# Rows of G for the first four chunks by three transfers, one gate range for them, and a new order of the first 830 steps

## The chip, the core and the metric

The kernel runs on one core of a Trainium2 chip. Its engines work side by side, each through its own queue in order: PE (TensorE) multiplies matrices, DVE (VectorE), ACT (ScalarE) and POOL (GpSimd) do element-wise work, SP issues most DMAs; ACT issues some. The metric is the device time of one execution in microseconds; less is better.

## The reference

Three stages follow each other. For 4 batches, 8 heads, 768 steps and head size 40, a recurrence with exponential gates:

```
m_new = max(f[t] + m, i[t]);  fs = exp(f[t] + m - m_new);  is = exp(i[t] - m_new)
C = fs*C + is * v[t] k[t]^T;  n = fs*n + is*k[t]
y[t] = sigmoid(o[t]) * (C q[t]) / max(|n . q[t]|, 1)
```

The outputs, 3072 tokens of 320 numbers, go through two feed-forward stages with 2048 hidden units: `h = x @ w_in; g = h*clip(h+3, 0, 6)/6; x = g @ w_out`, and the same with `g = max(h, 0)**2`. The result has 3072 x 320 numbers.

## The kernel before, in words

The recurrence is done in 12 chunks of 64 steps. A unit is one batch and one chunk; there are 48, and the first eight are chunks 0 and 1 of batches 0 and 1 and then of batches 2 and 3. For a unit, `at_load` fetches q and k transposed (`qkt`), k (`kI`) and v (`Z`); `at_S` (L431, L433) multiplies q with k into PSUM; `at_P` (L455) multiplies that by the gate weights W; `x_k` (L403, L406) scales k; `at_Y` (L473) multiplies with v and the carried state; `at_C` (L481) carries the state on; `at_n1`, `at_n2`, `at_n3` normalise and multiply by the sigmoid of the o gate (`o_load`, `o_sig`) into X.

W is exp(G[t] - G[s] + ...), with G the running sum of gate logs. A range of chunks goes through `gate_m` (a max-scan), `gate_g`, `gate_G` (a sum-scan), `gate_b` and `gate_bT` on 32 partitions, one for each batch and head. Before, the ranges are chunks 0-1, 2-3 and 4-11. For the first four chunks (units 0 to 15) G is split into two parts of 32-bit "r" format, high and low, in the tile Gp, and `w_pe` forms the exponent on PE: the first matmul (L353) writes the causal mask, the second (L355) adds, with `gb[:, c]` as stationary and R[b] as moving operand, the b terms through 64 rows that select the head (`head_rows`) and G through two rows of ones. R and gb lie in the tile `pre`. Each unit's two rows of R[b] are loaded by `at_gload`: two DMAs on ACT's queue, 32 in all for 16 units. `w_e` (L375) takes the exponential on ACT. Later units get W by a broadcast DMA from DRAM.

The feed-forward stages work in slots: `mm_A` (L619, eight matmuls of w_in into PSUM), `act1`, `act1b`, `act2`, `act2b` (L628 to L650: the activation and its split into a high part `gh` and a low part `gl`), then `mm_B` (L660). The first 16 slots take half the tokens each. X is transposed by `t_pe` (L595) and split by `t_hi`, `t_lo` into `xs`, and mm_A:0 needs the transposes of batches 0 and 1, that is units 0 to 3. The weights come as 64-bit floats: `w_load` (768 or 640 KB), `w_exp` (ACT), `w_b1`, `w_b2` (DVE), `w_hi` (ACT or DVE), `w_lo` (POOL or DVE).

The order of all of it is written out by hand in the text FIRST, step by step (`name:arguments`, and `@v`, `@g`, `@a` for DVE, POOL or ACT where a step may run on several); behind its last step a rule continues. Each engine runs its instructions in that order. Each DMA takes the next of eight completion lanes (DMAHW0 to 7) in turn and waits, on the queue of the engine that issues it, until the lane's last DMA has landed.

Of the kernel before, what the change touches and what calls it, by code (L numbers as in the profile page):

```python
# [38 lines left out]
w_e:2 w_b2:0,0 w_load:0,4 w_e:3 w_pe:4 x_k:2@v w_hi:0,0 w_pe:5 at_P:2,0 w_exp:0,2 w_lo:0,0 at_n1:1
at_Y:2 at_n2:1 at_load:5 w_e:5 at_n1:2 w_e:4 w_b1:0,2 w_exp:0,1 w_load:0,3 at_S:3 at_n2:2 x_k:3  # L40
at_gload:7 at_gload:6 at_gload:8 at_P:3,0 at_gload:9 at_C:2 at_n3:2 at_Y:3 at_load:6 at_n3:1
t_pe:0,0,0 at_n1:3 at_C:3 t_hi:0,0,0 at_n2:3 w_pe:6 w_load:0,6 at_n3:3 w_pe:7 w_exp:0,4 w_b2:0,2
w_e:6 t_lo:0,0,0 w_e:7 w_hi:0,2@v t_pe:0,0,1 at_gload:11 w_load:0,5 at_gload:10 w_b1:0,1 t_hi:0,0,1
t_lo:0,0,1 w_exp:0,3 w_lo:0,2@v mm_A:0 w_load:0,7 w_b2:0,1 mm_A:1 act1:0 w_b1:0,4 w_hi:0,1 at_S:4
act1b:0 x_k:4 act1:1 act2:0 act1b:1 w_lo:0,1 at_load:7 act2b:0 act2:1 act2b:1 w_exp:0,6 mm_A:2
at_P:4,0 w_load:0,8 mm_A:3 w_b2:0,4 act1:2 at_S:5 w_b1:0,3 w_hi:0,4 act1b:2 x_k:5 mm_B:0,1 act1:3
at_P:5,0 at_Y:4 w_exp:0,5 at_load:8 w_lo:0,4 act1b:3 mm_B:0,0 act2:2 at_n1:4 at_S:6 at_C:4 act2b:2
load_gates:1 act2:3 at_n2:4 x_k:6 w_exp:0,7 mm_A:4 at_P:6,0 at_load:9 w_b1:0,6 mm_B:1,0 act1:4
at_Y:5 w_b2:0,6 mm_B:1,1 w_load:0,10 at_n1:5 at_C:5 at_S:7 w_hi:0,6 x_k:7@v act2b:3 w_exp:0,8
w_lo:0,6 at_load:10 at_P:7,0 mm_A:5 act1b:4 w_pe:8 at_n2:5 act2:4 w_load:0,9 act1:5 act2b:4 at_Y:6  # L50
w_e:8 act1b:5 mm_A:6 w_b2:0,3 at_gload:12 at_C:6 at_n1:6 w_hi:0,3 at_S:8 w_load:0,12 at_n3:4 act1:6
at_n2:6 w_lo:0,3 x_k:8@a act1b:6 at_Y:7 at_P:8,0 at_n3:6@g at_n1:7 mm_B:2,0 mm_B:2,1 at_C:7@v
at_load:11 mm_B:3,1 w_exp:0,10 w_b1:0,5 t_pe:0,0,2 w_b2:0,5 mm_B:3,0 t_hi:0,0,2 at_n3:5 act2:5
w_load:0,11 w_hi:0,5 at_n2:7 at_n3:7 at_Y:8 act2:6 act2b:5 w_lo:0,5 w_exp:0,9 o_load:1 act2b:6
mm_A:7 at_C:8 t_lo:0,0,2 w_b1:0,7 t_pe:0,0,3 act1:7 mm_B:4,1 w_b2:0,7 w_exp:0,12 mm_B:4,0
w_load:0,13 mm_B:5,0 act1b:7 t_hi:0,0,3 mm_B:5,1 w_b1:0,8 w_hi:0,7 t_lo:0,0,3 act2:7 w_lo:0,7
act2b:7 mm_A:8 w_load:0,14 at_n1:8 at_n2:8 mm_A:9 w_exp:0,11 w_b2:0,8 act1:8 mm_B:6,1 act1:9
mm_B:6,0 act1b:8 w_hi:0,8 act1b:9 mm_B:7,0 gate_m:2 mm_B:7,1 o_load:2 act2:8 w_pe:9 act2:9 o_sig:1
act2b:8 w_lo:0,8 act2b:9 mm_B:8,3 mm_A:10 w_e:9 o_load:3 at_gload:13 gate_g:2 mm_A:11 w_exp:0,13
act1:10 mm_B:8,2 act1:11 act1b:10 at_n3:8@g mm_B:9,2 act1b:11 act2:10 mm_B:9,3 act2b:10 w_pe:10  # L60
w_exp:0,14 gate_G:2 mm_A:12 w_e:10 mm_B:10,3 act1:12 mm_B:10,2 at_gload:14 act2:11@v at_S:9 x_k:9
o_sig:2 act2b:11 act1b:12 mm_A:13 at_P:9,0 at_load:12 act2:12 act2b:12 mm_B:11,2 act1:13 w_b1:0,10
at_S:10 o_sig:3 act1b:13 x_k:10 mm_A:14 at_P:10,0 act2:13 at_load:13 act2b:13 mm_B:12,2 act1:14
mm_B:11,3 w_b2:0,10 mm_A:15 act1b:14 w_hi:0,10 gate_b:2 w_pe:11 act2:14 mm_B:12,3 w_e:11 at_Y:9
act2b:14 w_lo:0,10 o_load:5 act1:15 w_pe:12 at_gload:15 act1b:15 at_C:9 mm_A:16 at_n1:9 act2:15
act2b:15 w_e:12 w_b1:0,9 w_b2:0,9 mm_A:17 act1:16 w_load:0,15 gate_bT:2 w_hi:0,9 act1b:16 o_load:4
w_lo:0,9 at_S:11 act1:17 at_n2:9 mm_B:13,2 act1b:17 at_Y:10 x_k:11 at_P:11,0 mm_B:13,3 w_b1:0,12
at_C:10 at_load:14 at_S:12 act2:16 w_b1:0,11 act2b:16 x_k:12 mm_B:14,3 w_exp:0,15 mm_B:14,2
at_P:12,0 at_load:15 mm_A:18 act2:17 w_b2:0,12 act2b:17 w_hi:0,12 w_pe:13 at_n3:9 act1:18 mm_A:19
w_b2:0,11 w_e:13 act1b:18 w_lo:0,12 w_hi:0,11 at_n1:10 w_pe:14 act1:19 at_n2:10 mm_B:15,2 mm_B:16,2  # L70
w_e:14 act1b:19 w_lo:0,11 at_Y:11 w_pe:15 at_gload:16 at_n1:11 at_C:11 mm_B:15,3 w_add:16 w_e:15
mm_B:16,0 act2:18 mm_B:16,3 mm_B:16,1 at_n3:10 at_n2:11@a at_S:13 act2b:18 w_mask:16 w_b1:0,14
mm_A:20 at_P:13,0 x_k:13 w_e:16 w_b2:0,14 at_load:16 act2:19 at_Y:12 act1:20 act2b:19 mm_B:17,1
at_gload:17 at_C:12 at_S:14 x_k:14 at_n1:12 w_hi:0,14 at_n2:12 mm_B:18,1 at_n3:12 at_load:17
at_Y:13 at_P:14,0 w_lo:0,14 mm_B:17,0 act1b:20 at_C:13 at_gload:18 t_pe:0,1,0 at_n1:13 mm_B:17,2
t_hi:0,1,0@v mm_B:17,3 x_q:16 mm_B:18,2 t_lo:0,1,0 act2:20 mm_B:18,3 mm_B:19,3 act2b:20 w_add:17
mm_A:21 at_n3:11 at_n2:13 w_mask:17 mm_B:19,2 act1:21 at_n3:13 at_Y:14 act1b:21 w_add:18 w_e:17
t_pe:0,1,1 at_C:14 mm_A:22 at_n1:14 w_mask:18 t_hi:0,1,1@v at_n2:14@a t_lo:0,1,1 mm_B:18,0
w_b1:0,13 at_S:15 w_b2:0,13 act2:21 w_b1:0,15 mm_B:19,0 w_e:18 at_P:15,0 x_k:15 mm_B:19,1 act1:22
act2b:21 at_S:16 x_k:16 at_load:18 w_hi:0,13 at_Y:15 act1b:22 at_n3:14@g mm_A:23 at_P:16,0 act2:22  # L80
at_gload:19 at_P:16,1 at_C:15 at_load:19 at_n1:15 w_lo:0,13 at_n2:15 act2b:22 at_S:17 act1:23
at_gload:20 at_Y:16 w_b2:0,15 mm_B:20,2 at_C:16 x_q:17@v mm_B:20,0 w_hi:0,15 mm_B:21,0 at_n1:16
at_n3:15@g mm_B:20,3 at_n2:16 mm_B:21,2 at_P:17,0 w_lo:0,15 mm_B:20,1 at_P:17,1 mm_B:21,1 act1b:23
t_pe:0,1,2 mm_B:21,3 act2:23 x_k:17@v mm_B:22,1 t_hi:0,1,2 act2b:23 w_add:19 mm_B:22,2 at_load:20
at_Y:17 t_lo:0,1,2 w_mask:19 mm_B:22,3 at_gload:21 at_n1:17 at_C:17 t_pe:0,1,3 at_n2:17 mm_B:22,0
x_q:18 w_e:19 mm_B:23,0 t_hi:0,1,3 mm_B:23,1 evac:23,0 t_lo:0,1,3 mm_B:23,2 at_n3:17@g evac:23,1
mm_B:23,3 evac:23,2 mm_A:24 evac:23,3 x_k:18@v at_n3:16 x_q:19 mm_A:25 act1:24 act1b:24 x_k:19
act2:24 at_S:18 w_add:20 mm_A:26 act1:25 at_P:18,1 at_load:21 act1b:25 w_add:21 act2:25@v mm_A:27
act2b:24 act2b:25 act1:26 at_P:18,0 w_mask:20 mm_B:24,2 act1b:26 act1:27 at_gload:22 at_Y:18
w_mask:21 act2:26@v w_e:20 mm_B:25,2 at_C:18 act2b:26 at_S:19 w_e:21 mm_B:24,0 at_n1:18 x_q:20  # L90
at_load:22 mm_B:24,3 at_n2:18 mm_A:28 at_P:19,0 at_P:19,1 w_add:22 act1b:27 mm_B:24,1 x_k:20@v
at_gload:23 act1:28 mm_B:25,0 at_n3:18@g mm_B:25,3 act2:27 act1b:28 at_Y:19 act2b:27 at_S:20
at_C:19 at_n1:19 x_q:21 mm_B:26,0 qk_split:22 at_load:23 mm_A:29 mm_B:26,2 act1:29 at_P:20,1
w_mask:22 mm_B:26,3 at_n2:19 mm_B:27,3 w_add:23 w_e:22 act1b:29 mm_B:27,2 mm_A:30 at_P:20,0
at_gload:24 x_k:21@v qk_split:23 at_Y:20 at_S:21 at_C:20 mm_B:25,1 at_load:24 at_n1:20 at_n3:19@g
mm_B:26,1 act2:28 mm_B:27,1 at_P:21,1 mm_B:27,0 act2:29@v x_q:22 mm_A:31 at_n2:20 at_P:21,0
at_gload:25 act2b:28 at_S:22 act2b:29 act1:30 mm_B:28,3 act1b:30 w_mask:23 act1:31 mm_B:28,2
mm_B:28,0 qk_split:24 mm_A:32 w_e:23 mm_B:28,1 at_P:22,0 x_k:22 mm_B:29,1 mm_B:29,0 act2:30@v
w_add:24 mm_B:29,3 at_load:25 act1b:31 at_Y:21 act2:31 at_n3:20 mm_A:33 act2b:31 act2b:30
at_gload:26 t_pe:0,2,0 at_n1:21 w_mask:24 act1:32 mm_B:30,0 at_n2:21 mm_B:30,1 act1:33 x_q:23  # L100
act1b:32 mm_B:30,3 w_e:24 mm_B:31,0 at_C:21@v mm_A:34 at_n3:21 t_hi:0,2,0@v x_k:23 act1b:33
w_add:25 at_load:26 mm_B:31,1 t_lo:0,2,0 mm_B:31,3 at_Y:22 w_mask:25 at_S:23 at_n1:22 at_C:22
w_add:26 mm_A:35 w_e:25 at_n2:22 at_P:23,0 qk_split:25 at_gload:27 t_pe:0,2,1 mm_B:29,2 t_hi:0,2,1
mm_B:30,2 act2:32 mm_B:31,2 x_q:24@v at_Y:23 act2b:32 at_C:23 act2:33@v x_q:25 mm_B:32,2 act1:34
# [745 lines left out]
```

## Time and profile before

| what | value |
|---|---|
| runs, median (lowest to highest) | 859.5 us (857.76 to 860.44) |
| profiled execution, its span | 858.58 us, 856.8 us |
| PE busy | 820.4 us, 96% of the span |
| DVE, ACT, POOL busy | 534.0, 415.5, 205.8 us |
| HBM read and written | 58.36 and 4.00 MB |

The busy time of PE is near the span, so that the time of the kernel is PE's work plus what PE waits, and the places to look at are those where PE is idle or its clock is lowered. A wait that the profile shows on another engine counts only if PE's next instruction stands behind it.

### The profile page before, as it was taken

The page shows a single profiled execution, that of the slowest core. Times are in us where ns is not written, and L with a number is a line of the kernel's source. Part 1 is how long each engine was busy: PE and PEld are TensorE (multiplying, and loading weights), DVE is VectorE, ACT ScalarE, POOL GpSimd, SP SyncE. Part 2 cuts the span into 40 slices and gives each one's busy share as a digit, 9 for nine tenths or more (in the row PEclk, how much of TensorE's full clock was granted, in tenths as well). Part 3 has the DMA queues.
Part 4 walks back from the last instruction along what each step waited for, and adds up shares of the span by engine and source line. Part 5 has one row for each costly group of instructions (what it writes and reads, how often), then busy time and mean ns, then how long its engine had stood idle before and what let it go on. Part 6 is the DMA issues. An engine that isn't in the chain of part 4 may idle for free.

```text
span 856.8 us, 19209 instructions
## 1 busy us (share of the span) xinstructions
PE 820.4 (96%) x7968; PEld 724.2 (85%) x7968; DVE 534.0 (62%) x963; ACT 415.5 (48%) x727; POOL 205.8 (24%) x188
## 2 busy tenths in 40 slices
...
GB/s 193 185 139 314 41 148 90 66 138 79 91 83 107 99 92 116 83 105 62 2 37 157 188 160 1 1 31 1 1 32 1 31 1 1 31 1 1 31 1 31
DMA packets 29188, 63.66 MB, mean 74 GB/s; under 512 B 5261, under 2 KB 17613, under 8 KB 29101
## 3 DMA queue, kind: packets, MB, share of 16 engines
...
q8 instruction: 62, 1.02, 0.5%
...
q10 hardware_dynamic: 512, 0.07, 0.1%
HBM read 58.36 MB, written 4.00 MB: 73 GB/s over the span
## 4 chain that ended last, share of the span: by engine, by line
PE 83%; DVE 5%; DMA 4%; ACT 4%; issue 2%; SPq 2%; ACTq 0%; POOL 0%; POOLq 0%; DVEq 0%
PE hps L619 38%; PE acc L660 36%; PE Yp L473 3%; PE tp L595 2%; PE Sp L439 2%; DMA qkt<-in_qk 1%; DVE qs L417 1%; DMA rwi<-in_w1i 1%; ACT qs L415 1%; PE Sp L431 1%; PE Sp L433 1%; DMA rwo<-in_w1o 1%; DVE X L512 1%; DMA pre<-Gp 0%; DVE Xm L455 0%
## 5 line engine op out<-in xcount | busy, mean ns | idle before, releaser
L619 PE MATMUL hps<-xs,wi 128*128 128x512 f32 (+1 forms) x1600 | 392.1, 389 | 4.0 <-DVE gl L650 3.1
L660 PE MATMUL acc<-wo,gh 128*128 128x320 f32 x1536 | 349.1, 314 | 0.0
L619 PEld LDWEIGHTS hps<-xs,wi 128*128 128x128 f32 x1600 | 289.3, 192 | 54.4 <-DVE gl L650 3.5
L660 PEld LDWEIGHTS acc<-wo,gh 128*128 128x128 f32 x1536 | 259.3, 189 | 10.1
L660 PE MATMUL acc<-wo,gl 128*128 128x320 f32 x768 | 237.9, 310 | 0.0
L650 DVE TENSOR_TENSOR gl<-g,gh 128x512 fp32r<-128x512 f32 x176 | 128.2, 730 | 65.9 <-ACT gh L645 64.9
L640 DVE TENSOR_TENSOR g<-g 128x512 f32<-128x512 f32 x96 | 66.4, 692 | 127.6 <-ACT g L630 127.1
L660 PEld LDWEIGHTS acc<-wo,gl 128*128 128x128 f32 x768 | 144.6, 188 | 0.2
L628 ACT ACTIVATE g<-hps,three 128x512 f32<-128x512 f32 (+1 forms) x104 | 67.8, 654 | 152.5 <-PE hps L619 140.6
L645 ACT CAST gh<-g 128x512 fp32r<-128x512 f32 x168 | 104.1, 619 | 67.5 <-DVE g L640 53.3
L630 ACT ACTIVATE g<-hps 128x512 f32<-128x512 f32 x96 | 57.4, 598 | 151.5 <-PE hps L619 151.5
L637 DVE SCALAR_TENSOR_TENSOR g<-g,hps 128x512 f32<-128x512 f32 x80 | 54.8, 686 | 53.3 <-ACT g L628 53.0
L395 POOL TENSOR_TENSOR Xm<-qkt,W 40x512 f32<-40x512 f32 x29 | 38.3, 1321 | 111.8 <-ACT W L385 77.4
L580 POOL TENSOR_TENSOR wi<-wt,wi 128x768 fp32r<-128x768 f32 x15 | 29.7, 1979 | 128.5 <-ACT wi L575 125.5
L473 PEld LDWEIGHTS Yp<-Z,Xm 104*32 104x32 f32 (+1 forms) x3072 | 35.0, 109 | 20.4 <-issue 12.4
L473 PE MATMUL Yp<-Z,Xm 104*32 104x41 f32 (+1 forms) x3072 | 41.1, 208 | 6.9 <-DVE Xm L455 4.6
L417 DVE SCALAR_TENSOR_TENSOR qs<-qs,less,qkt 120x512 fp32r<-120x512 f32 x52 | 39.4, 799 | 11.1 <-ACT qs L415 11.0
L362 POOL TENSOR_TENSOR W<-W,bT 104x512 f32<-104x512 f32 x32 | 44.3, 1386 | 1.5 <-DMA W<-Gd 1.4
L406 POOL TENSOR_TENSOR Xm<-kI,W 104x320 f32<-104x320 f32 x37 | 33.6, 909 | 31.0 <-ACT W L375 21.0
L580 POOL TENSOR_TENSOR wo<-wt,wo 128x640 fp32r<-128x640 f32 x16 | 26.0, 1626 | 49.0 <-ACT wo L575 46.4
L512 DVE TENSOR_TENSOR X<-X,yt 64x320 f32<-64x320 f32 x39 | 32.6, 836 | 1.1
L481 ACT COPY Z<-Yp 40x328 f32<-40x328 f32 x41 | 17.4, 427 | 30.5 <-PE Yp L473 11.1
(102 smaller groups left out, 652.1 us busy)
## 6 DMA issues: line engine op xcount, KB each, us to landing
...
```

What stands on the lines that cost most here:

```text
L362: on("w_add", "g", u).tensor_tensor(out=W, in0=W, in1=bT[:, c - NC1, b * H:(b + 1) * H].unsqueeze(2).to_broadcast([KX, H, L]), op=ALU.add)
L417: nc.vector.scalar_tensor_tensor(out=y[0:KS, i], in0=y[0:KS, i].bitcast(F32), scalar=less[0:KS, i:i + 1], in1=x[0:KS, i], op0=ALU.mult, op ...
L473: nc.tensor.matmul(out=Yp[o:e, h, :], lhsT=Xm[:, h, o:e], rhs=Z[b][c % 2][:, h, :], start=True, stop=True)
L580: on("w_lo", "g", ph, i).tensor_tensor(out=w[:, 1], in0=f, in1=w[:, 0].bitcast(F32), op=ALU.subtract)
L619: nc.tensor.matmul(out=h, lhsT=w[:, hl, kk, o:o + P], rhs=t[:, xk, i0 * P:i1 * P], start=(i == 0), stop=(i == len(TERMS) - 1))
L628: nc.scalar.activation(out=g, in_=T["h", s], func=ACTF.Relu, bias=three)
L630: nc.scalar.activation(out=g, in_=T["h", s], func=ACTF.Relu)
L637: nc.vector.scalar_tensor_tensor(out=g, in0=r, scalar=6.0, in1=T["h", s], op0=ALU.min, op1=ALU.mult)
L640: nc.vector.tensor_tensor(out=g, in0=r, in1=r, op=ALU.mult)
L645: copy("act2", s)(out=gh, in_=g)
L650: nc.vector.tensor_tensor(out=gl, in0=g, in1=gh.bitcast(F32), op=ALU.subtract)
L660: nc.tensor.matmul(out=acc[i], lhsT=g[:, n], rhs=w[:, hl, m % MG, :], start=(m == 0 and q == 0), stop=(m == NM - 1 and q == 2))
```

## The change

Chunks 0 to 3 become one gate range (`cuts = [0, NC1, NC]` with NC1 = 4), so that the scans run once over 256 columns. Gp's two halves are stored to a DRAM tile Gd1 by two DMAs (`at_G:0,0` and `at_G:0,1`), and one DMA (`at_R:0`) loads all rows for all batches: R[b] has eight rows of G, high and low of four chunks, instead of two. The stationary operand selects the chunk: `gb` has a block with ones only in the two rows of its chunk, made by `const_o` from the identity. The 32 loads of `at_gload` for units 0 to 15 are gone. FIRST has 829 steps instead of 845, in a new order; it holds the same steps but for those of the gates.

```diff
-const_g load_gates:0 const_z:0 const_i at_load:0 head_rows:1 at_load:1 const_z:1 head_rows:0
+const_z:3 const_i load_gates:0 const_g const_k:0 const_m head_rows:2 const_z:1 w_load:0,4 const_z:0
...
+    Gd1 = dram.tile([NC1, 2, BH * L], F32, name="Gd1")
...
-    cuts = [0, 2, 4, NC]
+    cuts = [0, NC1, NC]
...
-    KW = 2 * BH + 2
+    KW = 2 * BH + 2 * NC1
...
-        nc.vector.memset(gb[2 * BH:KW].bitcast(F32), 1.0)
...
+        k = slice(2 * BH, KW)
+        nc.vector.tensor_tensor(
+            out=gb[k],
+            in0=ident[k, 2 * BH:KW:2].unsqueeze(2).to_broadcast([2 * NC1, NC1, KX]),
+            in1=ident[k, 2 * BH + 1:KW:2].unsqueeze(2).to_broadcast([2 * NC1, NC1, KX]),
+            op=ALU.add)
...
+    def at_G(r, i):
+        c0, c1 = cuts[r], cuts[r + 1]
+        nc.scalar.dma_start(
+            out=Gd1[c0:c1, i].rearrange("c (h l) -> c h l", l=L),
+            in_=Gp[:, i, c0 * L:c1 * L].bitcast(F32).rearrange("h (c l) -> h c l", l=L))
+
+    def at_R(r):
+        c0, c1 = cuts[r], cuts[r + 1]
+        k = 2 * BH + 2 * c0
+        nc.scalar.dma_start(
+            out=pre[k:k + 2 * (c1 - c0), 0:B].bitcast(F32),
+            in_=Gd1[c0:c1].rearrange("c i (b k) -> (c i) b k", b=B))
+
     def at_gload(u):
         b, c = units[u]
-        if u < U1:
-            for i in range(2):
-                nc.scalar.dma_start(
-                    out=R[b][2 * BH + i:2 * BH + i + 1].bitcast(F32),
-                    in_=Gp[b * H:(b + 1) * H, i, c * L:(c + 1) * L].bitcast(F32))
-            return
```

On ACT, the rows from the head rows to the first exponentials, before. CAST `pre<-gt` is gate_bT's copy, X_110 the o gate that the sigmoid takes, DMAHW and a number the lane that is waited for:

```order
3 L259 CAST pre<-ident 32x512 x8
4 L335 DMA pre<-Gp 1x8x64 [waits DMAHW6_49,DVE_49]
5 L335 DMA pre<-Gp 1x8x64 [waits DMAHW7_49,DVE_49]
6 L335 DMA pre<-Gp 1x8x64 [waits DMAHW1_49]
7 L335 DMA pre<-Gp 1x8x64 [waits DMAHW3_49]
8 L335 DMA pre<-Gp 1x8x64 [waits DMAHW4_49]
9 L335 DMA pre<-Gp 1x8x64 [waits DMAHW5_49]
10 L308 CAST pre<-gt 32x2x64 [waits DVE_49]
11 L335 DMA pre<-Gp 1x8x64 [waits DMAHW6_49]
12 L335 DMA pre<-Gp 1x8x64 [waits DMAHW7_49]
13 L519 ACT_TABLE_LOAD
14 L519 ACTIVATE X_110<-X_110 128x1280 [waits DMAHW0_49]
```

The same piece of ACT now; rwi is a weight as loaded, L572 is w_exp, L393 the exponential of w_e, L593 w_hi, L499 at_C:

```order
3 L269 CAST pre<-ident 32x512 x6
4 L344 DMA Gd_117<-Gp 32x4x64 [waits DMAHW3_49,DVE_49]
5 L344 DMA Gd_117<-Gp 32x4x64 [waits DMAHW5_49,DVE_49]
6 L351 DMA pre<-Gd_117 8x2048 [waits DMAHW5_49,DMAHW3_49,DMAHW0_49]
7 L319 CAST pre<-gt 32x4x64 [waits DVE_49]
8 L572 ACTIVATE rwi_142<-rwi_142 128x768 [waits DMAHW2_49]
9 L572 ACTIVATE rwi_168<-rwi_168 128x768 [waits DMAHW6_49]
10 L393 ACTIVATE W<-Wp 104x512 [waits PE_49] x2
11 L593 CAST wi_255<-wt 128x768 [waits DVE_49,Activation_49]
12 L393 ACTIVATE W<-Wp 104x512 [waits PE_49] x2
13 L499 COPY Z_103<-Yp 40x328 [waits DVE_49,PE_49]
14 L393 ACTIVATE W<-Wp 104x512 [waits PE_49,Pool_49]
```

Eight small loads, of which the fourth and later wait for lanes of other loads, became two stores and a load that waits for both; the sigmoid moved from ahead of the first exponential to behind the fifth (row 17 now).

On SP, the first loads after the gates, now (kI, qkt and Z belong to a unit, rwi and rwo are weights, X_110 is the o gate):

```order
3 L560 DMA rwi_142<-in_w1i 128x768
4 L333 DMA qkt<-in_qk 40x1024
5 L339 DMA kI_99<-in_kn 64x320
6 L340 DMA Z_102<-in_va 64x328
7 L560 DMA rwi_168<-in_w1i 128x768
8 L333 DMA qkt<-in_qk 40x1024
9 L339 DMA kI_100<-in_kn 64x320 [waits DMAHW0_49]
10 L340 DMA Z_104<-in_va 64x328 [waits DMAHW1_49]
11 L333 DMA qkt<-in_qk 40x1024 [waits DMAHW2_49]
12 L339 DMA kI_101<-in_kn 64x320 [waits DMAHW4_49]
13 L340 DMA Z_103<-in_va 64x328 [waits DMAHW6_49]
14 L533 DMA X_110<-in_og 128x4x320 [waits DMAHW7_49]
```

Before, three units' loads and the o gate stood ahead of the first weight; now a weight is first, a second one follows the first unit, and the third unit waits for their lanes (2 and 6).

On PE, the last rows before the first feed-forward matmul, before (Z_105 is unit 3's v, tp a transpose of X, Wp w_pe's sum, hps mm_A's):

```order
145 L473 MATMUL Yp<-Z_105,Xm 32x41 x3
146 L473 MATMUL Yp<-Z_105,Xm 8x41
147 L595 MATMUL tp<-ident,X_110 128x128 x3
148 L353 LDWEIGHTS identb
149 L353 MATMUL Wp<-maskb,identb 104x512
150 L355 MATMUL Wp<-pre 104x512
151 L353 LDWEIGHTS identb
152 L353 MATMUL Wp<-maskb,identb 104x512
153 L355 MATMUL Wp<-pre 104x512
154 L595 MATMUL tp<-ident,X_110 128x128 x3
155 L619 MATMUL hps<-xs,wi_386 128x256 x16
```

And now, where Z_106 is unit 4's v:

```order
180 L491 MATMUL Yp<-Z_106,Xm 32x41 x3
181 L491 MATMUL Yp<-Z_106,Xm 8x41
182 L613 MATMUL tp<-ident,X_110 128x128 x3
183 L371 LDWEIGHTS identb
184 L371 MATMUL Wp<-maskb,identb 104x512
185 L373 MATMUL Wp<-pre 104x512
186 L613 MATMUL tp<-ident,X_110 128x128 x3
187 L637 MATMUL hps<-xs,wi_255 128x256 x16
```

Eight w_pe stand before the first feed-forward matmul in both; now also at_S and at_Y of unit 4.

## Rows read from the trace of the kernel before

**Rows 1.** The page: busy time, share of the span, instructions of each engine.
```profile
PE 820.4 (96%) x7968; PEld 724.2 (85%) x7968; DVE 534.0 (62%) x963; ACT 415.5 (48%) x727; POOL 205.8 (24%) x188
```

**Rows 2.** Busy by stretch; last columns granted clock, DMA share, GB/s.
```profile
0.00:46.60 46.60, 24.87 (x407) 16.09 (x407) 23.50 (x67) 21.12 (x34) 6.73 (x20) 1.00 0.59 191
46.60:240.00 193.40, 183.97 (x2766) 158.73 (x2766) 153.06 (x306) 107.54 (x210) 82.19 (x74) 0.97 0.40 118
240.00:857.00 617.00, 611.58 (x4796) 549.33 (x4796) 357.41 (x593) 286.86 (x485) 116.92 (x94) 1.00 0.18 52
```

**Rows 3.** Timeline of PE: start, us, operation, [idle before, releaser].
```profile
17.04 0.76 PE L355 MATMUL Wp<-pre 66*104 66x512 f32 x1 [8.28 <-DVE pre L309]
...
24.35 0.37 PE L431 MATMUL Sp<-qkt 40*64 40x64 f32 x1
...
26.25 1.31 PE L473 MATMUL Yp<-Z,Xm 104*32 104x41 f32 x64
27.49 0.67 PE L353 MATMUL Wp<-maskb,identb 64*104 64x512 bf16 x1
...
28.77 0.67 PE L353 MATMUL Wp<-maskb,identb 64*104 64x512 bf16 x1
...
36.63 1.32 PE L473 MATMUL Yp<-Z,Xm 104*32 104x41 f32 x64 [0.81 <-DVE Xm L455]
...
45.16 0.88 PE L595 MATMUL tp<-ident,X 128*128 128x128 f32 x3 [2.58 <-DVE xs L606]
46.60 4.03 PE L619 MATMUL hps<-xs,wi 128*128 128x256 f32 x16 [0.57 <-ACT xs L599]
...
57.68 0.80 PE L473 MATMUL Yp<-Z,Xm 104*32 104x41 f32 x64
...
80.95 2.08 PE L619 MATMUL hps<-xs,wi 128*128 128x256 f32 x16
```

**Rows 4.** Timeline of ACT; columns as rows 3.
```profile
8.10 8.24 ACTq L335 DMA_DIRECT2D pre<-Gp  x5
16.38 0.30 ACT L308 CAST pre<-gt 32x128 fp32r<-32x128 f32 x1 [9.15 <-DMA pre<-Gp]
...
17.73 1.28 ACT L519 ACT_TABLE_LOAD   x1 [1.05 <-DMA pre<-Gp]
...
21.60 1.08 ACT L375 ACTIVATE W<-Wp 104x512 f32<-104x512 f32 x2
...
34.25 7.25 ACTq L335 DMA_DIRECT2D pre<-Gp  x6
```

**Rows 5.** The chain that ended last, up to 48 us: start, duration, what.
```profile
1.20 0.41 SPq L224
...
7.91 7.77 DMA rwi<-in_w1i
...
36.18 4.25 DMA pre<-Gp
```

**Rows 6.** Timeline of DVE: the gate work of the first range.
```profile
3.65 0.47 DVE L266 TENSOR_TENSOR_SCAN gt<-gt 32x128 f32<-32x128 f32 x1
...
4.82 0.28 DVE L275 TENSOR_TENSOR gt<-gt 32x128 f32<-32x128 f32 x1
...
5.70 0.22 DVE L291 CAST Gp<-gt 32x128 fp32r<-32x128 f32 x1
```

**Rows 7.** DVE, groups by form: xcount | busy us, mean ns | idle before.
```profile
L266 DVE TENSOR_TENSOR_SCAN X<-X,X 32x512 f32<-32x512 f32 x1 | 1.3, 1267 | 0.0
```

**Rows 8.** PE's waits: for whom, us in total, times, longest.
```profile
PE hps L619 <- DVE gl L650: 3.1, 2, 1.6
```

**Rows 9.** Busy by stretch around two low clocks; columns as rows 2.
```profile
75.00:80.00 5.00, 3.63 (x17) 3.63 (x18) 4.45 (x9) 1.89 (x4) 0.51 (x1) 0.66 1.02 338
90.00:95.00 5.00, 3.43 (x29) 2.90 (x30) 3.42 (x7) 3.45 (x8) 1.00 (x2) 0.82 0.08 14
95.00:100.00 5.00, 5.00 (x54) 4.55 (x52) 2.01 (x4) 3.93 (x6) 0.00 (x0) 0.50 0.24 70
```

More of the change, by code (lines that the diff above doesn't have):

```diff
@@ L39 @@
[L39 to L104, printed above, removed]
@@ L111 @@
-at_n2:24 act1:39 mm_B:36,3 at_P:25,0 at_n3:24@g mm_B:37,3 mm_A:40 act1b:39 x_q:26@v x_k:26@a
-act2b:38 mm_B:36,2 mm_B:36,0 mm_B:37,0 mm_B:37,2 mm_B:36,1 mm_B:37,1 act2:39@v act2b:39
+const_z:3 const_i load_gates:0 const_g const_k:0 const_m head_rows:2 const_z:1 w_load:0,4 const_z:0
+const_l const_z:2 head_rows:3 const_k:1 const_k:2 at_load:0 gate_m:0 head_rows:0 gate_g:0
+w_load:0,0 gate_G:0 const_o at_G:0,0 at_G:0,1 at_load:1 gate_b:0 at_R:0 at_S:0 head_rows:1@g
+gate_bT:0 at_load:2 w_exp:0,4 o_load:0 w_b1:0,4 w_pe:0 w_exp:0,0 w_b2:0,4 w_pe:1 w_e:0 w_b1:0,0
@@ new lines @@
+w_load:0,1 at_S:1 w_b2:0,0 w_e:1 w_pe:2 at_P:0,0 x_k:0 w_hi:0,0 w_pe:3 at_load:3 at_P:1,0 x_k:1
+at_Y:0 w_e:2 w_lo:0,0 w_e:3 w_pe:4 at_n1:0 at_load:4 at_S:2 at_C:0 at_n2:0 w_e:4 at_Y:1 w_hi:0,4
+at_P:2,0 w_load:0,7 w_pe:5 o_sig:0 x_k:2@v at_C:1@v w_pe:6 at_n1:1 at_Y:2 w_load:0,2 at_n2:1 at_S:3
+x_k:3 at_n1:2 at_C:2 at_n3:1@g w_exp:0,1 at_P:3,0 w_e:6 at_n3:0 at_Y:3 w_load:0,3 at_n2:2 at_S:4
+x_k:4 at_n1:3 at_n3:2 w_exp:0,7 at_P:4,0 at_C:3 at_n2:3 at_Y:4 at_load:5 w_e:5 w_lo:0,4@v
+t_pe:0,0,0 at_C:4 w_pe:7 w_b1:0,1 at_load:6 w_exp:0,2 t_hi:0,0,0@v at_n3:3@g w_e:7 t_lo:0,0,0
```

113 lines of the change are left out of this document (88 added, 25 removed).

## The prediction

> **What bounds the kernel now.** I read the page first, then the busy time by stretch, then PE's waits, the chain that ended last, and the timelines of ACT, DVE and PE up to the first feed-forward matmul. The page has PE busy for 820.4 us of the span, 96% [rows 1]: whatever the change does to other engines, it can only pay where PE waits or runs slowly. The stretches say where that is. Up to 46.6 us, where L619 starts, PE is busy 24.87 us, so 21.7 idle; from there to 240 us, about where the written list ends, 183.97 of 193.4, so 9.4 idle, at a mean granted clock of 0.97; the 617 us behind that lose 5.4 [rows 2]. All matmuls stay, so the end moves with what the first two stretches lose.
>
> The first stretch is held by ACT and its DMA queue, not by work. PE waits 8.28 us for its first L355 matmul, at 17.04 [rows 3]; the cast that feeds it stands on ACT at 16.38 behind five DMA issues that took 8.24 us [rows 4]. The chain names what held them: the landing of an `rwi` load, 7.77 us, until 15.7 [rows 5]. A weight load has nothing to do with a row of G but the completion lane, of which the order shows eight in turn. Then ACT loads a table for the sigmoid at 17.73, runs it, loads the other table back, and takes its first exponential at 21.60 [rows 4]. It happens once more: six issues from 34.25 take 7.25 us [rows 4], the chain ends in a `pre<-Gp` landing of 4.25 us [rows 5], the second transpose of X starts at 45.16 after 2.58 us of waiting, and L619 at 46.60 [rows 3].
>
> **The change part by part.** *Gates in one range.* DVE's scan of 128 columns starts at 3.65 and takes 0.47 us, the one of 512 takes 1.27 [rows 6, 7]; that is 2.07 ns a column, 0.74 for 256. The second scan is counted at the same 0.74. The two additions of 0.28 are at most doubled (1.12 together), the copy of the high half goes from 0.22 to at most 0.43 [rows 6], and 0.4 stands for a one-column copy, a memset and gaps. The high half is ready at 3.65 + 0.74 + 0.74 + 1.12 + 0.43 + 0.4 = 7.1 us. The first store issues there, the second an issue of 0.63 later, at 7.7; its low half is ready by then. The new product that fills `gb` (const_o) and gate_bT's cast and subtraction are hidden: they run while the round trip below is under way.
>
> *Three transfers for 32.* The new price is that round trip: the load waits until both stores have landed, w_pe:0 waits for the load, and on ACT gate_bT's cast, two w_exp and the exponentials stand behind the waiting issue. No row shows a store that something waits for. Bounds for one such transfer, issue to landing: the scan at 3.65 used gates whose issue began at 1.20, so at most 2.45 us [rows 5 to 7]; the `pre<-Gp` landing in the chain took 4.25 [rows 5]. Two in series put T, the start of w_pe:0's second matmul, between 7.7 + 4.9 = 12.6 and 7.7 + 8.5 = 16.2 us. The queues carry two weight loads and an o_gate load at that time, as they carried loads in the 4.25 us case, so I take the value nearer to that row: T = 14.8, against 17.04 now.
>
> The Trainium skill (DMA: Bandwidth & Descriptors, Anatomy of one DMA) puts a fixed 2.0 us on a transfer, most of it the receipt of the write, with HBM the slowest target; that speaks against a bounce through DRAM, yet by its figure T would be an estimated 11.8 us, 3 us better than my sum. The chain's 4.25 us [rows 5] is twice the page's price, and I keep to the row.
>
> *Loads moved on SP.* Two weight loads now go out ahead of most unit loads, and unit 2's q/k and v wait for their lanes. The landing of such a load took 7.77 us with all that was queued before it [rows 5]; issued near 1.7 and 3.9 us they are in by 12, and PE wants unit 2 at about T + 9 = 24. Hidden; if not, at_S:2 pays the difference.
>
> *The new order up to mm_A:0.* The sigmoid with its two tables goes behind the exponentials of units 0 to 4. I add PE's list from T with this trace's durations: a w_pe 1.28 (27.49 to 28.77), an at_S 1.90 (24.35 to 26.25), an at_Y 1.24 (26.25 to 27.49), a transpose 0.88 [rows 3]. From T to mm_A:0 stand 0.7 for the rest of w_pe:0, seven w_pe (9.0), at_S 1 to 4 (7.6), at_Y 0 to 4 (6.2), two transposes (1.8), at units 3 and 4 a wait each of 0.75 for at_P, which follows its own at_S, and 0.5 for the copy between the last transpose and L619. That is 0.7 + 9.0 + 7.6 + 6.2 + 1.8 + 1.5 + 0.5 = 27.3 us, against 29.56 now (17.04 to 46.60). mm_A:0 starts at 14.8 + 27.3 = 42.1, 4.5 us earlier. DVE's list at the last transpose (at_P, a product, a w_lo, a w_b1, t_hi, t_lo) I take as just in time; if it is late, the 2.58 us wait of today is the price [rows 3].
>
> *Unit 4 is done before mm_A:0*, where now its at_S follows mm_A:1 and its at_Y comes at 57.68. Those 1.90 and 0.80 us [rows 3] leave the later stretch: 2.7.
>
> *From mm_A:0 to the list's end* the same matmuls stand in another order, and the later G issues leave ACT. DVE takes on work: six high halves of the 16 half slots instead of one, and four weight halves. It is busy 153.06 of 193.4 us there [rows 2]. The most to be won is what is lost now, 9.4 us idle and 0.03 x 193.4 = 5.8 of clock; as much can be lost again. Nothing in the order tells which waits come out of it: I take 0, the stretch as it is, and keep 15 us either way as the ends.
>
> *Sum.* Profiled execution 858.58 us (a span of 856.8 and 1.8 around it), minus 4.5, minus 2.7: 851.4. The median shown, 859.5, is 0.9 above the profiled one; on its footing 852.3. Forecast: 852 us.
>
> **The rivals.** *A: the bounce eats it.* Each transfer takes 6 us, T is 7.7 + 12 = 19.7 and mm_A:0 comes at 47.0. For it: weight packets are queued right ahead of the stores. Against it: 4.25 is the longest landing of this kind in the chain [rows 5]. Unit 4's 2.7 less 0.4 stay: 857.2, no change.
>
> *B: the clock rises earlier.* Up to 55 us PE has the pace of the lower level (1.2 GHz): sixteen L619 matmuls last 4.03 us at 46.60 and 2.08 at 80.95, an at_Y 1.31 at 26.25 and 0.80 at 57.68 [rows 3]. The granted-clock column says 1.00 there, so the durations tell. PE had no gap from 24.35 until the 0.81 us before 36.63 [rows 3] and did not rise; the gapless stretch of the new order is 27 us long. Should it rise halfway, its second half (13.6) takes 6.8 less, and the first 9 us of slots 4.5 less: 852 - 11 = 841. The Trainium skill (TensorE: Matmul & The Clock Gate, Part 1) says that the default state is throttled and sustained activity releases it; by that alone B would be likely. The trace agrees only in part: the gapless small matmuls up to 36 us released nothing.
>
> *C: the middle gets worse, and the result is slower.* One mechanism: between mm_A:1 and mm_A:24 PE catches up with DVE, waits for `gl`, and the clock falls to 1.2 GHz behind the wait. The trace has it twice: 3.1 us of waiting in two pieces [rows 8], and in the stretches from 75 and 90 us idle PE (1.37 and 1.57) with granted clocks of 0.66, 0.82 and 0.50 [rows 9]. The clock's part is (0.34 + 0.18 + 0.50) x 5 = 5.1 us, so 8.2 in all, 4.1 an episode. For it: the new list has mm_B on the heels of mm_A (A0, A1, B0, A2, B1), so DVE's splits come due sooner, and there are more. Against it: unit 4 is out of the way, and DVE is 79% busy [rows 2]. Two extra episodes take the whole 7.2 us; three give 852 + 12.3 = 864.
>
> *D: the middle gets better.* ACT's issues and lane waits between slots go, and half of the 15 us comes back: 844.5.
>
> **How the numbers follow.** The forecast with its own range (T between 12.6 and 16.2, and two or three microseconds in the middle): 847 to 856.5, chance 0.52. A 0.11, B 0.07, C 0.18, D 0.12. Within 0.3% (2.6 us) a measurement of this kernel can't tell a change from none, so faster is below 857 and slower above 862. Faster: 0.52 + 0.07 + 0.12, less 0.01 for the edge, 0.70; same: A and a C of two episodes, 0.14; slower 0.16. The range goes from 843 (B and the better half of D lie below) to 861 (most of C lies above).
>
> **What would show it.** Right: the first gate matmul of the second kind at 12.6 to 16.2 us; on ACT no idle stretch over 4 us that ends in a DMA, but the one for the stores; the sigmoid's table behind five exponentials; the first matmul of mm_A:0 at 40 to 44 us, and from T to there no PE wait over 1 us. Wrong in the round trip: that gate matmul after 17 us, released by the load. Wrong by C: `gl` at the head of PE's waits with over 6 us, and over three five-microsecond stretches up to 120 us with a granted clock under 0.9. Wrong by B: at_Y units of 0.8 us before mm_A:0. The prediction falls as a whole if mm_A:0 comes 4 us earlier and the end does not.

## The result and the profile after

The changed kernel takes 849.66 us (median of 4 runs, 848.42 to 851.42) against 858.63 (857.76 to 860.44) for the kernel before on the same chip: a ratio of 0.9894 (95% interval 0.9868 to 0.9921), or 9 us. The forecast was 852. The two steps that were to bring it did not: the first feed-forward matmul, announced 4.5 us earlier, came 4.0 us later, and the stretch behind it, taken as unchanged but for one unit, became 13.4 us shorter.

The first row is the page's line of busy time after, which answers to [rows 1]: PE has 4.6 us less to do and the span is 9.4 us shorter (847.4 after 856.8).

```profile
PE 815.8 (96%) x7968; PEld 720.5 (85%) x7968; DVE 534.4 (63%) x957; ACT 425.8 (50%) x773; POOL 203.9 (24%) x189
```

To see where, I cut both spans at two places: the start of mm_A:0 (46.60 before, 50.6 after), and ACT's first evacuation of a finished output block (157.3 before, 147.9 after). Busy time by stretch, before, with the granted clock in the third column from the end:

```profile
46.60:157.30 110.70, 103.98 (x1725) 89.67 (x1726) 86.91 (x181) 67.89 (x134) 47.62 (x41) 0.95 0.45 139
157.30:856.00 698.70, 691.58 (x5839) 618.40 (x5838) 423.56 (x716) 326.51 (x562) 151.49 (x128) 1.00 0.20 56
```

The same view after, with two short stretches beside [rows 9]:

```profile
0.00:50.60 50.60, 28.23 (x502) 19.09 (x502) 24.97 (x58) 21.77 (x33) 11.54 (x25) 1.00 0.58 173
50.60:147.90 97.30, 94.86 (x1547) 81.73 (x1548) 85.95 (x181) 67.54 (x142) 43.22 (x38) 0.98 0.48 154
147.90:847.00 699.10, 692.65 (x5921) 619.71 (x5920) 423.52 (x720) 336.44 (x599) 149.13 (x126) 1.00 0.20 57
75.00:80.00 5.00, 3.31 (x45) 2.70 (x33) 4.80 (x9) 3.76 (x8) 1.00 (x1) 0.82 0.90 270
80.00:85.00 5.00, 5.00 (x31) 4.32 (x30) 3.90 (x8) 4.03 (x8) 1.47 (x3) 0.84 0.10 19
```

The last stretch is equal in both (698.7 and 699.1), the first is 4.0 longer, the middle one is 110.7 before and 97.3 after. So the whole gain lies within 100 us behind mm_A:0. The rows let it be split. PE's idle time there goes from 110.70 - 103.98 = 6.7 to 2.4 us (-4.3). The clock's loss, one minus the mean granted clock, goes from 0.05 x 110.7 = 5.5 to 0.02 x 97.3 = 1.9 (-3.6). The matmuls in it fall from 1725 to 1547, which is the work of two units. Unit 4 is now done ahead of it, the prediction's 2.7 us. A later unit's at_S and at_Y (16 and 64 matmuls, 0.7 and 0.8 us of PE) now stand behind it; the last stretch takes them in without growing, as its idle time falls from 7.1 to 6.5 us. Together they are 4.2 us that were moved and not saved. The rest, about 1.3, goes with PE's low pace, which ends sooner after mm_A:0. PE's timeline before and after shows that, at 6 us behind mm_A:0 in both:

```profile
52.45 3.59 PE L619 MATMUL hps<-xs,wi 128*128 128x256 f32 x16
```

```profile
50.63 3.94 PE L637 MATMUL hps<-xs,wi 128*128 128x256 f32 x16 [0.57 <-ACT xs L617]
56.64 1.12 PE L637 MATMUL hps<-xs,wi 128*128 128x256 f32 x8
```

Sixteen such matmuls still last 3.59 us before; eight last 1.12 after, which is 2.24 for sixteen.

PE's waits in the middle stretch (for whom, us in total, times, longest), which answer to [rows 8]:

```profile
PE hps L637 <- ACT xs L617: 1.1, 2, 0.6
PE Yp L491 <- issue: 0.8, 1, 0.8
PE hps L637 <- DVE gl L668: 0.4, 1, 0.4
```

The wait for `gl`, 3.1 us before, is 0.4 now.

Why mm_A:0 is late stands in the chain of waits (start, duration, what) and on ACT and PE (timeline), beside [rows 3 to 5]:

```profile
8.98 5.17 DMA Gd<-Gp
...
14.25 6.67 DMA pre<-Gd
```

```profile
8.04 1.25 ACTq L344 DMA_DIRECT2D Gd<-Gp  x2
14.25 0.52 ACTq L351 DMA_DIRECT2D pre<-Gd  x1
14.81 0.40 ACT L319 CAST pre<-gt 32x256 fp32r<-32x256 f32 x1 [8.84 <-DMA Gd<-Gp]
```

```profile
21.06 0.72 PE L373 MATMUL Wp<-pre 72*104 72x512 f32 x1 [10.49 <-DMA pre<-Gd]
...
49.19 0.88 PE L613 MATMUL tp<-ident,X 128*128 128x128 f32 x3 [0.44 <-DVE xs L624]
```

The stores are issued from 8.04 us and the second lands at 14.15; the load goes at 14.25 and lands at 20.92. The round trip takes 12.9 us, so w_pe:0's second matmul, the prediction's T, starts at 21.06.

### The profile page after: what moved, and what is told of

It reads as the page before. It is cut to its first block, busy times and chain, and to the rows that moved or that the text cites. A ratio compares the mean times of both kernels' runs of the same rounds, so it can differ in the third digit from the quotient of the medians.

```text
span 847.4 us, 19202 instructions
## 1 busy us (share of the span) xinstructions
PE 815.8 (96%) x7968; PEld 720.5 (85%) x7968; DVE 534.4 (63%) x957; ACT 425.8 (50%) x773; POOL 203.9 (24%) x189
## 3 DMA queue, kind: packets, MB, share of 16 engines
q8 instruction: 62, 1.02, 0.5%
## 4 chain that ended last, share of the span: by engine, by line
PE 87%; DVE 6%; ACT 2%; issue 2%; DMA 1%; POOL 0%; ACTq 0%; DVEq 0%; POOLq 0%
PE hps L637 39%; PE acc L678 37%; PE Yp L491 4%; PE tp L613 2%; PE Sp L457 2%; PE Sp L449 1%; PE Sp L451 1%; DVE gl L668 1%; PE Wp L373 1%; DVE qs L435 1%; DMA pre<-Gd 1%; PE Wp L371 1%; ACT qs L433 1%; DMA Gd<-Gp 1%; ACT g L646 0%
## 5 line engine op out<-in xcount | busy, mean ns | idle before, releaser
L663 ACT CAST gh<-g 128x512 fp32r<-128x512 f32 x173 | 107.1, 619 | 69.0 <-DVE g L658 53.4
L413 POOL TENSOR_TENSOR Xm<-qkt,W 40x512 f32<-40x512 f32 x28 | 36.5, 1303 | 111.0 <-ACT W L403 79.5
L598 POOL TENSOR_TENSOR wi<-wt,wi 128x768 fp32r<-128x768 f32 x14 | 26.8, 1914 | 106.6 <-ACT wi L593 99.7
L598 POOL TENSOR_TENSOR wo<-wt,wo 128x640 fp32r<-128x640 f32 x14 | 23.6, 1683 | 32.1 <-ACT wo L593 29.3
L530 DVE TENSOR_TENSOR X<-X,yt 64x320 f32<-64x320 f32 x37 | 29.7, 802 | 1.1
L449 PE MATMUL Sp<-qkt 40*64 40x64 f32 x256 | 22.4, 250 | 8.0 <-DMA qkt<-in_qk 8.0
```

Source lines behind the costliest of these rows:

```text
L598: on("w_lo", "g", ph, i).tensor_tensor(out=w[:, 1], in0=f, in1=w[:, 0].bitcast(F32), op=ALU.subtract)
L663: copy("act2", s)(out=gh, in_=g)
```

## The experiments

All were timed in alternation with the kernel before (its medians there were 857.0 to 858.6), in three groups on different chips: e1 to e4, e5 to e7, e8. Kernels of different groups are best compared by their ratios. "Middle" is the time from mm_A:0 to the first evacuation; it, T and mm_A:0 are those of the profiled run, whose own time stands beside the median. Line numbers of variants can differ by a few.

| kernel | median us | profiled run | ratio and interval | T | mm_A:0 | middle |
|---|---|---|---|---|---|---|
| before | 858.63 | 858.58 | | 17.04 | 46.60 | 110.7 |
| after | 849.66 | 849.22 | 0.9894, 0.9868 to 0.9921 | 21.06 | 50.63 | 97.3 |
| e1, rows alone | 851.81 | 853.80 | 0.9933, 0.9912 to 0.9953 | 18.98 | 41.54 | 107.4 |
| e2, order alone | 855.56 | 859.80 | 0.9982, 0.9967 to 0.9996 | 18.77 | 49.50 | 107.4 |
| e3, quiet | 844.38 | 844.44 | 0.9854, 0.9836 to 0.9872 | 16.61 | 46.57 | 97.0 |
| e4, unit 4 late | 853.40 | 854.75 | 0.9952, 0.9937 to 0.9966 | 20.22 | 48.01 | 105.5 |
| e5, quieter | 844.88 | 844.44 | 0.9848, 0.9823 to 0.9874 | 14.01 | 45.51 | 98.0 |
| e6, direct | 842.70 | 844.51 | 0.9817, 0.9793 to 0.9841 | 14.51 | 43.03 | 100.5 |
| e7, rows on POOL | 855.75 | 856.20 | 0.9958, 0.9939 to 0.9977 | 18.74 | 50.07 | 102.8 |
| e8, spread | 843.81 | 842.82 | 0.9838, 0.9814 to 0.9861 | 14.35 | 43.37 | 97.3 |

**One half of the change at a time.** e1 has the three transfers and the single gate range, in the order of before:

```
-const_i load_gates:0 ... at_gload:0 ... gate_m:1 gate_g:1 ...
+const_i const_m const_o load_gates:0 ... at_G:0,0 at_G:0,1 at_R:0 ...
```

> The three transfers and the single gate range with the order of before (its at_gload steps dropped, the stores and the load where at_gload:0 stood). Theory O, the gain is the new order's and lies in the slots behind mm_A:0: the round trip again waits for the queued loads, the second gate matmul (L371 here for the sum with G) starts at 19 to 22 us, mm_A:0 comes at 44 to 49, and the time is within 4 us of before, 854 to 860. Theory R, the gain comes from ACT being rid of the issues and lane waits of 29 DMAs: PE's stretch from mm_A:0 to the first evacuation shrinks by 8 us or more, and the time is 848 to 852.

e2 has the new order and the single range, with the rows of G fetched by 32 loads on ACT's queue:

```
-at_G:0,0 at_G:0,1 ... at_R:0
+at_gload:0 at_gload:1 at_gload:4 at_gload:5
-w_e:0
+w_e:0 at_gload:2
...
```

> The new order and the single gate range, but the rows of G by two small loads for each of the 16 units on ACT's queue, as before: four units' loads where the one load stood, each later one behind the exponential that frees its row. Theory O: the order carries the gain, 848 to 853 us. Theory R: 856 us or more, with ACT waiting for lanes behind the exponentials, 5 us or more in all before 70 us.

Neither half is the change, and neither theory comes as it was put. The rows alone bring 0.67%, and bring it at the start: mm_A:0 comes 5.1 us earlier, before theory O's 44, and the middle is 3.3 shorter, where theory R asked for 8. Of these 8.4 us 3.5 are lost again between the first evacuation and the end of the span (703.0 us against 699.5), where PE waits 3.2 for DVE's g. PE's waits of e1 still have the one that the middle of before had:

```profile
PE hps L635 <- DVE gl L666: 3.1, 2, 1.6
```

The order alone brings 0.18%, a median between the two announced ranges: mm_A:0 is 2.9 late, and the middle is 3.3 shorter, less than the 4.2 of the two units that have left it here too. It does take the `gl` wait away (0.7 is left), but new waits stand in its place, most of them for ACT, on whose queue the row loads are. Its waits in the middle, and three stretches of low clock:

```profile
PE Wp L359 <- ACT W L381: 2.2, 2, 1.9
PE hps L625 <- ACT xs L605: 2.0, 2, 1.5
PE Yp L479 <- issue: 1.9, 1, 1.9
PE hps L625 <- DVE gl L656: 0.7, 1, 0.7
```

```profile
75.00:80.00 5.00, 5.00 (x86) 4.76 (x85) 4.34 (x7) 2.25 (x5) 3.01 (x2) 0.66 0.92 288
110.00:115.00 5.00, 3.05 (x11) 2.04 (x10) 1.59 (x4) 4.97 (x13) 0.18 (x1) 0.79 0.22 59
115.00:120.00 5.00, 5.00 (x76) 4.04 (x76) 4.86 (x11) 2.95 (x9) 2.52 (x2) 0.50 0.00 0
```

e2's profiled run was its longest, 4.2 us above the median, and e1's is 1.9 above its own. If all of that lay in the middle, e2's would be 7.5 shorter than before's and e1's 5.2. Without the 4.2 us of moved work the change has 9.2 us in the middle to explain; e1 gives 3.3 to 5.2 of them, e2 at most 3.3 and by its rows none. That speaks for halves that do more together than apart, but it is not shown: by the totals, 0.67% and 0.18% add up to 0.85% of 1.06%, a difference that the intervals cover.

**e7** gives e2's later row loads to POOL, to see how much of that is ACT's issuing:

```
-nc.scalar.dma_start(
+(nc.scalar if c < 1 else nc.gpsimd).dma_start(
```

> The kernel with the new order alone (rows by 32 loads), with the loads of chunks 1 to 3 issued by POOL instead of ACT. Theory I (what spoils the middle stretch when the rows come by 32 loads is their issue on ACT: 0.64 us each, two to a unit, with waits of 0.8 and 0.9 us behind a load): mm_A:0 at 49.5 as there, but mm_A:0 to the first evacuation 97 to 101 us instead of 107.4, total 846 to 850. Rival W (it is the landing of the rows, or the late load of o_gate, whoever issues): 105 to 109 and 853 to 857.

The profile gives a middle of 102.8, between the two announced ranges, but the total is the one that rival W announced: 855.75 us, a ratio of 0.9958 (0.9939 to 0.9977) beside e2's 0.9982 (0.9967 to 0.9996). By the ratios that is 2 us of the 7.5 between e2 and the change, with intervals that overlap: ACT's issuing is at most a smaller part of the price. With POOL issuing, PE still waits 3.2 us for a row ahead of mm_A:0 (at 35.98) and 1.3 us for `gl` in the middle, and its granted clock is 0.71 from 80 to 85 us. Of the 5.5 us by which e7's middle exceeds after's, 1.6 are idle time and 1.2 the granted clock; the rest goes with the low pace, which lasts longer: 7.7 us behind mm_A:0, e7's eight matmuls take 1.70 us where after's took 1.12 at 6 us:

```profile
57.74 1.70 PE L625 MATMUL hps<-xs,wi 128*128 128x256 f32 x8
```

Why the row loads should do that, and whether o_gate's late load has a part, I did not settle.

**e4** undoes one move of the new order, unit 4 before mm_A:0:

```
-at_S:4 x_k:4 ... at_P:4,0 ... at_Y:4 ... at_C:4 ... at_load:7 ... mm_A:0 at_n1:4 ... mm_A:1
+mm_A:0 ... mm_A:1 at_S:4 x_k:4 at_P:4,0 at_load:7 ... mm_B:0,1 at_Y:4 at_C:4 at_n1:4 ...
```

> The changed kernel with unit 4's at_S, at_P and x_k behind mm_A:1 and its at_Y, at_C and normalisation behind the first mm_B, as in the order of before (unit 7's loads move with them). My term for unit 4: mm_A:0 comes about 3 us earlier and the 2.7 us come back in the slots, the time 850 to 853. Rival: it is dearer, since the chain at_S, at_P, at_Y then stands between the first slots and PE waits for it, 853 to 857.

mm_A:0 starts 2.6 us sooner, and the middle is 8.2 longer; the profiled span is 5.6 longer, the median 3.7 (5.0 by the ratios). That is more than the unit's own 2.7, and most of the extra is the clock: after short waits of PE, the one of 0.80 at 53.79 and the one of 1.40 at 74.88, it is at the lower of its two levels (1.2 GHz). Waits in the middle, then windows:

```profile
PE Yp L490 <- issue: 1.4, 1, 1.4
PE hps L636 <- ACT xs L616: 1.1, 2, 0.6
PE Sp L448 <- DVE Xm L472: 0.8, 1, 0.8
```

```profile
48.01:153.50 105.49, 101.55 (x1643) 87.46 (x1644) 86.66 (x181) 67.70 (x143) 43.78 (x39) 0.94 0.48 146
55.00:60.00 5.00, 5.00 (x78) 4.33 (x78) 2.79 (x10) 1.34 (x2) 0.00 (x0) 0.50 0.66 198
75.00:80.00 5.00, 5.00 (x61) 4.79 (x55) 2.84 (x7) 1.64 (x3) 1.45 (x1) 0.55 1.01 419
```

The mean of 0.94 over 105.5 us is a loss of 6.3, against 1.9 in after: 4.4 of the 8.2. PE's idle time, 3.9 against 2.4 us, is 1.5 more.

**The price of the round trip.** e3 takes traffic away from it: o_gate's first load and block 1 of the weights go out behind it.

```
-at_load:2 w_exp:0,4 o_load:0 w_b1:0,4 ... w_b1:0,0 w_load:0,1 at_S:1 ... at_load:3 at_P:1,0
+at_load:2 w_exp:0,4 w_b1:0,4 ... w_b1:0,0 at_S:1 ... at_load:3 o_load:0 w_load:0,1 at_P:1,0
```

> The changed kernel with two loads of 640 KB (o gate of the first pair, weight 0,1) issued behind unit 3's loads instead of ahead of the rows' load, so that fewer bytes are queued during the round trip. Theory Q, the round trip waits for what is queued on the DMA engines: the first gate matmul with G starts at 13 to 16 us instead of 21.1, mm_A:0 5 to 7 us earlier than 50.6, and if the end follows the time is 843 to 846. Theory F, the bounce through DRAM has a fixed price of 5 to 6 us a transfer: the matmul stays at 19 to 22 us and the time at 849 to 851. Theory M, the slots behind mm_A:0 are held by DVE and not by their start: the matmul comes early and the time stays at 848 to 851.

T falls from 21.06 to 16.61, just outside theory Q's 13 to 16 and far below theory F's 19, and what T gains is passed on, against theory M: mm_A:0 is 4.1 us earlier, the first evacuation 4.3, the span 4.7. e5 moves block 0 of the weights (768 KB) behind the round trip too:

```
-w_load:0,0 gate_G:0 ... at_load:3 o_load:0 w_load:0,1 at_P:1,0
+gate_G:0 ... at_load:3 o_load:0 w_load:0,1 w_load:0,0 at_P:1,0
...
```

> The quiet kernel (o_gate's first load and block 1 of w_in behind the round trip) with block 0 of w_in moved behind it too, its widening and rounding a few steps later. Theory Q (a small transfer lands when the big loads queued before it have drained): 768 KB at the 300 to 400 GB/s of this stretch are 2 to 2.6 us, so the stores land at 11 to 12 instead of 13.76, w_pe:0's second matmul starts at 14 to 15 instead of 16.6, and, if block 0 is not itself late, mm_A:0 at 44 to 45 instead of 46.57 and the total is 842 to 843. Rival F (the price of a transfer does not hang on the queue): 16.6, 46.6 and 844.4 as in the quiet kernel. Rival L (block 0 is now the late one): w_pe:0 early, but mm_A:0 waits for block 0's upper half, total 846 or more.

The chain of waits of e3, and that of e5:

```profile
8.07 5.59 DMA Gd<-Gp
13.76 2.72 DMA pre<-Gd
```

```profile
9.02 2.10 DMA Gd<-Gp
11.18 2.69 DMA pre<-Gd
```

The same 32 KB store and 64 KB load cost 5.17 and 6.67 us in after, 5.59 and 2.72 with the two loads behind them gone, 2.10 and 2.69 with block 0 gone as well. That is theory Q as it was put: a small transfer on ACT's queue pays for what SP has queued on the same engines, and each load taken away shortened the transfer beside it alone. Block 0 cost the store 3.5 us, more than the 2 to 2.6 reckoned. But e5's total did not follow: T is 2.6 earlier, mm_A:0 1.1, the total the same. From T to mm_A:0 PE needs 31.5 us instead of 30.0, with a wait of 1.98 for ACT's W at 30.88. ACT's timeline shows W behind block 0's work, whose load lands at 26.8:

```profile
26.80 0.90 ACT L571 ACTIVATE rwi<-rwi 128x768 f32<-128x768 f32 x1 [5.71 <-DMA rwi<-in_w1i]
...
29.38 0.83 ACT L592 CAST wi<-wt 128x768 fp32r<-128x768 f32 x1 [1.22 <-DVE wt L583]
30.23 0.60 ACT L392 ACTIVATE W<-Wp 104x512 f32<-104x512 f32 x1
```

So block 0 became the late one, as in theory L, but by way of W and at a smaller price.

**e6** leaves the bounce out and keeps e3's order:

```
-at_G:0,0 at_G:0,1
+at_G:0,0
...
-    out=Gd1[c0:c1, i] ... in_=Gp[:, i, c0 * L:c1 * L]
-    out=pre[k:k + 2 * (c1 - c0), 0:B] ... in_=Gd1[c0:c1]
+for c in range(c0, c1):
+    for j in range(2):
+        (nc.scalar, nc.sync)[j].dma_start(out=pre[k:k + 1, 0:B], in_=Gp[:, j, c * L:(c + 1) * L])
```

> The quiet kernel with no bounce through DRAM: the eight rows of the first four chunks go from Gp straight to their rows by eight loads of one row for all four batches, four from ACT's queue and four from SP's. Issues of 0.64 us each as the 2 KB loads of before had, four on each engine, end at about 10.6. Theory Q (one transfer instead of two, each waiting for what is queued): landing at 13.5 to 14.5, so w_pe:0's second matmul at 14 to 15 instead of 16.6 and the total 842 to 843. Rival S (the loads behind SP's big loads wait longest, or one row is slow to move): 16.6 or later, total 844.4 or more.

T is 14.51 although four such issues take 5.10 us on ACT, 1.28 each, twice what I had reckoned; the last transfer takes 1.86 in the chain. mm_A:0 is at 43.03, the earliest of the new order. This is the best kernel of the study by its median: 842.70 us, some 7 below the changed kernel, though its interval overlaps those of e3, e5 and e8. Yet its first evacuation, 143.55, is where e3's (143.58) and e5's (143.46) are. Three kernels with mm_A:0 at 46.57, 45.51 and 43.03 meet at one time: what the start gains is given back in the middle. PE's idle time and clock loss there are together 3.3 us in e3, 4.8 in e5 and 7.1 in e6. PE's timeline of e6 shows two stops that are not at any semaphore ("issue"), and its windows what follows:

```profile
63.99 0.35 PE L488 MATMUL Yp<-Z,Xm 104*8 104x41 f32 x17 [1.12 <-issue]
...
70.93 0.28 PE L488 MATMUL Yp<-Z,Xm 104*8 104x41 f32 x9 [1.62 <-issue]
```

```profile
60.00:65.00 5.00, 3.86 (x151) 3.19 (x140) 3.36 (x12) 3.97 (x6) 1.76 (x2) 1.00 0.98 389
65.00:70.00 5.00, 4.31 (x93) 3.98 (x88) 4.35 (x7) 3.40 (x7) 2.93 (x2) 1.00 1.01 387
70.00:75.00 5.00, 3.50 (x23) 3.00 (x23) 4.30 (x10) 3.16 (x7) 0.09 (x1) 0.65 0.32 85
```

The DMA share (next to last column) is 0.98 and 1.01 while PE stops, and the clock falls behind the second stop.

**e8** takes two weight loads out of that queue, to 8 us later:

```
-w_load:0,14 ... w_load:0,13 ... w_load:0,12 ... at_load:10 ... at_load:11
+w_load:0,14 ... at_load:10 ... at_load:11 w_load:0,13 w_load:0,12
```

> The direct kernel with the loads of two w blocks (w_load:0,13 and w_load:0,12, 1.4 MB) moved from before at_load:10 to behind at_load:11, some 8 us later. In the direct kernel PE stops in the middle of the small matmuls of at_Y for 1.12 and 1.62 us at 63 and 69, on nothing that its semaphores show, while the DMA engines are busy 0.97 to 1.05 of the time, and its granted clock is 0.5 from 72 to 78; that is where its earlier start of mm_A:0 is given back. Theory D (PE's instruction stream comes late while the loads fill the DMA engines): with 1.4 MB less in the queue the stops in at_Y between 60 and 75 fall below 0.5 us together, the clock stays at 1.00, the first evacuation comes at 139 to 141 instead of 143.55 and the total is 838 to 841. Rival V (the stops have nothing to do with the loads): they stay at 1 to 2.7 us, evacuation at 143.5, total 842 to 843. Rival B (the two blocks are now late): ACT waits for rwi or rwo at 80 to 82, total 843 or more.

Theory D asked for less: the second stop is gone, the first stays (1.38 us, which by its size alone would fit rival V too; the blocks issued before the two moved ones still fill its queue, a DMA share of 0.96 from 60 to 65), and the clock holds, though PE now waits 1.14 us for DVE's xs at 72.22:

```profile
64.08 0.35 PE L488 MATMUL Yp<-Z,Xm 104*8 104x41 f32 x17 [1.38 <-issue]
```

```profile
65.00:70.00 5.00, 5.00 (x108) 4.52 (x103) 4.35 (x8) 3.12 (x7) 2.85 (x2) 1.00 0.82 232
70.00:75.00 5.00, 3.30 (x20) 2.51 (x19) 4.80 (x12) 3.80 (x8) 0.19 (x1) 1.00 0.62 253
```

The first evacuation comes at 140.65, 2.9 us before e6's, as theory D had it. The total does not show it: 843.81 and 842.70 can't be told apart, 1.2 us come back behind the evacuation (841.0 - 140.65 = 700.35 against 842.7 - 143.55 = 699.15), and e6's profiled run, 844.51, was one of its longer ones.

## Why the prediction came out where it did

The time was right within 2.4 us by luck: the working was not. Two terms, the start of mm_A:0 and the middle, were off by 8.5 and 10.7 us with opposite signs.

- *Gates in one range*: right. The scans took 0.74 and 0.68 us, the high half was ready at 6.9 (7.1 in the sum), the low half at 7.3. But the store, counted at 7.1, went at 8.04.
- *The round trip* is the step that failed first. I bounded one transfer by 2.45 and 4.25 us, took the value nearer to 4.25, and held the upper end for a bound because the row behind it had traffic too. The two transfers took 5.17 and 6.67, by e3 and e5 because of what SP had queued. The rival was in the text (A, 6 us each, T 19.7, mm_A:0 at 47.0); its reason against, that 4.25 was the longest landing in the chain, said nothing about another queue length. With a quiet queue e5 gives a T of 14.0, the forecast's 14.8. The Trainium skill (DMA: Bandwidth & Descriptors, Anatomy of one DMA) has a fixed 2.0 us for one transfer: e5's 2.10 and 2.69 are near it, after's 6.67 is three times as much. The Trainium skill gives that figure for DMAs on GpSimd's path, and these stand on ACT's queue. (The prediction's estimate of T by it, 11.8, should read 7.7 + 4.0 = 11.7.) The prediction's own sign for this error came: the gate matmul after 17 us, released by the load.
- *From T to mm_A:0*: 29.57 us instead of 27.3. The list of work was right; the waits were 3.9 us (1.18 and 0.85 in at_Y on "issue", 0.87 for at_P, 0.44 and 0.57 at the end) instead of the 2.0 counted, and one was over the 1 us that the prediction allowed. The last transpose waits 0.44, so DVE was just in time there, as assumed.
- *SP's moved loads*: hidden, as said. No PE wait behind T is for q, k or v.
- *Unit 4*: the mechanism was right and the price too small. Undoing it lost 3.7 us by the medians, 5.0 by the ratios, as its late place also costs waits and clock.
- *The middle at 0, with 15 us either way* is the second step that failed. It was rival D (half of the 15 us) with more than its price: 13.4 measured, of which 4.2 are the two units moved out of it and 9.2 are gain. Its reason, that ACT's issues go, is at most a part: e7 took them from ACT, and its middle is still 5.5 us longer than after's. What is seen to go is PE's wait for DVE's `gl`, 3.1 to 0.4, on which I had rival C speak the other way: the new order made DVE's splits come in time, not late (e1, without it, still waits 3.1). Low clock stood behind that wait and goes in part. C's reading of it was too simple, though: ahead of the fall at 75 us PE had stopped twice, and once for something else.

```profile
74.07 0.81 PE L473 MATMUL Yp<-Z,Xm 104*32 104x41 f32 x64 [1.26 <-issue]
```

- *B, the clock*: the pace rose sooner, but after mm_A:0, not before it: 6 us behind its start the matmuls are fast, where in before they were not. In the one profile of each kernel this goes with the rows and not with the order: e1, with before's order, has it too (sixteen matmuls in 2.18 us at 47.05), and e2 and e7, with the new order and the 32 loads, do not (eight still take 1.63 us at 57.12 and 1.70 at 57.74). Why stays open.

So A and D happened together, and a forecast between them was hit by their sum, which is luck. I had given each a chance as if only one could come.
